# Warm-up matmuls in three groups of fixed size ahead of the first tiles of a fused attention and gated-FFN kernel

## The chip, the cores and the metric

One core of one Trainium2 chip. Kernels are compared only within the same rounds. The metric is the device time of one execution in microseconds (us). The profile's "span" of the same execution is about 1.7 us shorter than its time (562.7 and 564.47 us for the profiled execution of the kernel before), so the two are never mixed below.

## The reference

```python
xn = layernorm(x)                                   # x: 1 x 2048 x 576, bf16
s  = window_attention(xn, wqkv) @ wo                # 32 heads of 18, window 256
h  = sigmoid(xn @ w_gate) * (xn @ w_up)             # 576 -> 4608
g  = silu(h @ w_down)                               # 4608 -> 576
out = x + s * g
```

## The kernel before

The program is a list of operations with estimated durations; a greedy scheduler orders them for each engine, and the order is then emitted. The tokens come in four chunks of 512. In the first chunk, each block of 128 rows goes through this chain: DMA of x, statistics and normalisation (VectorE, with one power on GpSimd), PE transposes, a copy out of PSUM (ScalarE for the first three blocks, VectorE for the fourth). "F tiles" are the gate/up matmuls. The first two F tiles are cut into four parts of 128 columns, one for each block of rows, so that they can start before the whole chunk is there; all later F tiles have 512 columns.

While x and the first weights travel, PE runs filler matmuls on zeros, so that its clock is fast when real work comes. In the trace of before the filler pairs start 427 ns apart until 6.95 us, where the clock record goes to full speed, and 216 ns apart after it:

```python
NWARM = 36
FIRST_SLACK_NS = -900.0     # correction of the estimated landing of the first weights
TURN_NS = 215.0             # part of the estimate of each probability-value product
...
h = self.pool_f.hold()
w = None
for i in range(NWARM):
    def f_warm(eng):        # one "pair": two matmuls of 64 rows x 512 columns, started within 6 ns in the trace
        return pair(eng, self.halves(h, NT), lambda r, t: zero[r, :],
                    lambda r, t: zero[r, None, :].broadcast_to([SW, NT // P, P]), True, True)
    w = op("PE", 427 if i < 11 else 216, f_warm, f"warm:{i}", deps=[z], prio=4, acq=None if i else h, odeps=[w])
    w.filler = h
    h.release(w)
```

```python
# build_ln, first chunk: the transposes of one block of rows and the copy out of PSUM
tr = op("PE", KB * 29.5, f_tr, f"tr:{st}", deps=[ap, dup, self.op_ident, war], prio=0, acq=h)
...
xe = op(eng, ..., f_xe, f"xe:{st}", deps=[tr], prio=0)

# build_ffn, first chunk: two F tiles in four parts each
for ft, h in enumerate(hs):
    u = None
    for part in range(len(PARTS[ft])):
        lo = gate_up(ft, h, 0, None if part else h, part, [u])
        u = gate_up(ft, h, 1, None, part, [lo])

# schedule(): fillers that are left when the first F part is placed are dropped
if o.name.startswith("f1"):
    for d in [d for d in ops if d.filler is not None and d.idx < 0]:
        ...
```

So the number of fillers that are really emitted is a result of the scheduler's estimates: wherever it believes that PE would be idle, it puts one in. It came out as 13 pairs, then 8, then 2.

The softmax here doesn't subtract the row's maximum and nothing guards it: scores larger than these inputs give would overflow.

## Time and profile before

| | |
|---|---|
| time, 3 executions | 562.57, 562.66, 563.74 us |
| time of the profiled execution | 564.47 us (span 562.7 us) |
| PE busy | 556.2 us |

The profile's page of the kernel before: the span, PE's busy time and instruction count, the instruction queue of the DMA, and the chain of waits by engine.

```profile
span 562.7 us, 19207 instructions
...
PE 556.2 (99%) x8314; PEld 337.2 (60%) x8314; DVE 334.7 (59%) x793; ACT 271.5 (48%) x379; POOL 210.9 (37%) x358
...
q8 instruction: 65, 1.06, 0.8%
...
PE 98%; DVE 1%; issue 0%; DVEq 0%
```

PE is the bound. Fillers count as busy, though, so the page alone cannot show what they cost. For that one reads the order of events at the start. The timeline of PE in the kernel before; the columns are start, duration of the run of like instructions, operation, output and inputs, shape, count, and idle time before it with its releaser:

```profile
1.05 5.73 PE L109 MATMUL ps<-hT 64*128 64x512 bf16 x26 [1.05 <-DVE small L434]
6.57 0.48 PE L545 MATMUL ps<-ident,xnr 64*128 64x64 bf16 x10
6.86 1.93 PE L109 MATMUL ps<-hT 64*128 64x512 bf16 x16
8.62 0.31 PE L545 MATMUL ps<-ident,xnr 64*128 64x64 bf16 x10
8.77 0.59 PE L109 MATMUL ps<-hT 64*128 64x512 bf16 x4
9.20 0.22 PE L109 MATMUL ps<-xnT,wgr 64*128 64x128 bf16 x2
...
10.22 0.31 PE L545 MATMUL ps<-ident,xnr 64*128 64x64 bf16 x10
...
13.22 0.22 PE L109 MATMUL ps<-xnT,wgr 64*128 64x128 bf16 x2
13.28 0.56 PE L109 MATMUL ps<-xnT,wgs 64*128 64x128 bf16 x14
15.08 0.46 PE L109 MATMUL ps<-xnT,wgs 64*128 64x128 bf16 x10 [1.25 <-issue]
15.36 0.40 PE L109 MATMUL ps<-xnT,wgr 64*128 64x512 bf16 x2
```

`ps<-hT` are the fillers (26, 16 and 4 matmuls: 13, 8 and 2 pairs), `ps<-ident,xnr` the transposes, `ps<-xnT,...` the F tiles. The normalised rows of the first block were ready at 5.68 us and transposed at 6.57; the second at 7.29 and 8.62. The first F tile's weights had landed at 7.77 and it started at 9.20. And a wait of 1.25 us, put down to "issue", stands in the middle of a run of F matmuls. The waits of PE in the same trace (total, times, longest):

```profile
PE ps L109 <- issue: 1.2, 1, 1.2
PE ps L109 <- DVE small L434: 1.1, 1, 1.1
```

### The profile page before, as it was taken

How to read it: one execution, taken by the hardware profiler on the slowest of the kernel's cores; microseconds unless marked ns; L12 is line 12 of the kernel's file. 1: busy time of each engine (PE TensorE's matmuls, PEld its weight loads, DVE VectorE, ACT ScalarE, POOL GpSimd, SP SyncE). 2: the span in 40 equal slices, each digit the busy share in tenths (PEclk: the TensorE clock that was granted, in tenths of full speed). 3: DMA queues.
4: the chain of work that ended last, by engine and by line, in shares of the span. 5: the costliest groups of instructions: out<-in, count | busy, mean ns of one | idle time of the engine just before them, and what ended most of it. 6: DMA issues, size and time to landing. Idle time of an engine off the chain costs nothing.

```text
span 562.7 us, 19207 instructions
## 1 busy us (share of the span) xinstructions
PE 556.2 (99%) x8314; PEld 337.2 (60%) x8314; DVE 334.7 (59%) x793; ACT 271.5 (48%) x379; POOL 210.9 (37%) x358
## 2 busy tenths in 40 slices
PE   8999999999999999999999999999999999999997
PEld 5454454677775454565877566555477754444786
DVE  5467778778576876735785773586656133333133
ACT  2235565554556556556555645765754133223011
POOL 4565357664356635404675540366330100000000
PEclk9999999999999999999999999999999999999999
DMA  8976999631215455326411233444521026552010
GB/s 234 286 205 145 275 207 282 175 87 43 76 34 148 133 148 142 109 84 123 102 55 35 81 111 104 117 143 142 168 62 37 22 75 179 166 151 67 1 44 23
DMA packets 113323, 67.81 MB, mean 121 GB/s; under 512 B 18476, under 2 KB 111372, under 8 KB 113240
## 3 DMA queue, kind: packets, MB, share of 16 engines
q1 hardware_dynamic: 105816, 60.68, 39.4%
q0 software_dynamic: 7424, 5.92, 4.0%
q8 instruction: 65, 1.06, 0.8%
q14 instruction: 18, 0.15, 0.1%
HBM read 55.15 MB, written 2.36 MB: 102 GB/s over the span
## 4 chain that ended last, share of the span: by engine, by line
PE 98%; DVE 1%; issue 0%; DVEq 0%
PE ps L109 94%; PE ps L746 3%; DVE o2T L772 0%; DVE ot L764 0%; DVE s_attn L997 0%; DVE o L768 0%; DVE thf L1002 0%; DVE v_aug L644 0%; PE ps L545 0%; DVE xf L1007 0%; DVE ot L767 0%; DVE xnT L533 0%; DVE hT L433 0%; DVEq L1159 0%; DVE small L434 0%
## 5 line engine op out<-in xcount | busy, mean ns | idle before, releaser
L109 PE MATMUL ps<-xnT,wgs 64*128 64x512 bf16 (+1 forms) x2400 | 285.6, 368 | 1.3 <-issue 1.2
L696 ACT ACTIVATE expr<-ps 128x1024 bf16<-128x1024 f32 (+2 forms) x160 | 156.8, 980 | 86.7 <-PE ps L109 86.1
L109 PEld LDWEIGHTS ps<-xnT,wgs 64*128 64x128 bf16 x2400 | 113.8, 94 | 118.2 <-issue 1.4
L109 PE MATMUL ps<-wd_sb,hT 64*128 64x288 bf16 (+2 forms) x2448 | 154.3, 276 | 0.0
L892 DVE SCALAR_TENSOR_TENSOR hT<-tring,ps 128x512 bf16<-128x512 bf16 x144 | 98.2, 684 | 90.4 <-ACT tring L889 87.8
L889 ACT ACTIVATE tring<-ps 128x512 bf16<-128x512 f32 x144 | 85.8, 597 | 115.9 <-PE ps L109 114.2
L109 PEld LDWEIGHTS ps<-wd_sb,hT 64*128 64x128 bf16 x2448 | 113.1, 94 | 27.7
L265 POOL DMA_DIRECT2D qk<-qd x160 | 82.6, 523 | 109.0 <-PE ps L109 99.8
L709 DVE TENSOR_TENSOR expr<-expr,mask 128x256 bf16<-128x256 bf16 (+2 forms) x232 | 62.9, 302 | 53.6 <-ACT expr L696 53.0
L661 POOL TENSOR_SCALAR kx<-kprev,small 128x256 bf16<-128x256 bf16 x64 | 61.8, 974 | 32.1 <-PE ps L109 31.3
L265 POOL DMA_DIRECT2D oT<-o2T x72 | 37.0, 521 | 61.6 <-DVE o2T L772 52.3
L109 PE MATMUL ps<-qk,kx 64*128 64x320 bf16 (+4 forms) x736 | 59.8, 251 | 0.0
L109 PE MATMUL ps<-xnT,wgr 64*128 64x512 bf16 (+1 forms) x300 | 55.9, 368 | 0.3
L109 PEld LDWEIGHTS ps<-qk,kx 64*128 64x128 bf16 x736 | 32.1, 94 | 25.6 <-DVE hT L892 1.4
L109 PE MATMUL ps<-xnT,wqk 64*128 64x512 bf16 x256 | 32.7, 377 | 0.0
L764 DVE STREAM_TRANSPOSE ot<-ps 128x512 f32<-128x512 f32 x32 | 22.5, 702 | 13.3 <-PE ps L746 13.3
L987 ACT ACTIVATE thf<-ps 128x576 bf16<-128x576 f32 (+3 forms) x22 | 11.4, 520 | 35.5 <-PE ps L109 35.0
L583 DVE CAST qd<-ps 128x1024 bf16<-128x1024 f32 (+1 forms) x20 | 22.2, 1114 | 6.5 <-PE ps L109 6.3
L661 DVE TENSOR_SCALAR kx<-qk,small 128x512 bf16<-128x512 bf16 x64 | 22.5, 378 | 3.4 <-PE ps L109 3.1
L772 DVE STREAM_TRANSPOSE o2T<-o 128x512 bf16<-128x512 bf16 x32 | 22.8, 712 | 1.1
L817 ACT ACTIVATE s_attn<-ps 128x576 bf16<-128x576 f32 x16 | 9.9, 649 | 27.9 <-PE ps L109 27.9
L109 PEld LDWEIGHTS ps<-xnT,wgr 64*128 64x128 bf16 x300 | 15.0, 94 | 13.4 <-issue 1.1
(64 smaller groups left out, 305.3 us busy)
## 6 DMA issues: line engine op xcount, KB each, us to landing
wgs<-in_B_w_gate_dram SPq DMA_DIRECT2D x72, 256.0 KB, 3.3
wgs<-in_B_w_up_dram SPq DMA_DIRECT2D x72, 256.0 KB, 3.9
wd_sb<-in_B_w_down_dram SPq DMA_DIRECT2D x9, 576.0 KB, 6.0
qk<-qd POOLq DMA_DIRECT2D x100, 36.0 KB, 2.2
wgr<-in_B_w_gate_dram SPq DMA_DIRECT2D x36, 64.0 KB, 2.2
wgr<-in_B_w_up_dram SPq DMA_DIRECT2D x36, 64.0 KB, 2.3
xf<-in_A_x_dram SPq DMA_DIRECT2D x16, 144.0 KB, 2.3
out_dram<-xf SPq DMA_DIRECT2D x16, 144.0 KB, 1.8
```

Of the source, the lines that this page charges most:

```text
L109: res = eng.matmul(outs[i], lhs(ROWS[t], i), rhs(ROWS[t], i), start=start, stop=stop, tile_position=(64 * t, 0))
L265: o = self.op(eng, DMA_ISSUE_NS[eng], lambda e: e.dma_start(dst, src), name, deps, prio, nbytes=nbytes)
L583: return eng.tensor_copy(dst, self.both(h, n))
L661: return e.tensor_scalar(self.kx[:, sx, pos:pos + n_ // SW, t, :], src.rearrange("p (s k) -> p s k", k=SW), self.half[:, t:t + 1], None, A ...
L696: return eng.activation(self.expr[:, se, :, lo * SW:NT], self.both(h, NT)[:, :, lo * SW:NT], ACTF.Exp, scale=SM_SCALE)
L709: return eng.tensor_tensor(e_, e_, m_, ALU.mult)
L746: res = eng.matmul(outs[i][p0:p0 + VH, cols], self.v_aug[ROWS[i], o:o + VH], self.expr[ROWS[i], se, t, cols], start=n == 0, stop=n == len( ...
L764: return e.transpose(self.ot1[:, p1, :], self.halves(hp, NT)[i])
L772: t2 = op("DVE", dve_ns(NT), lambda e, p2=p2, p3=p3: e.transpose(self.o2T[:, p3, :], self.o2[:, p2, :]), f"ot2:{c}:{pr}:{i}", deps=[on, d3 ...
L889: th = op("ACT", act_ns(NT), lambda e: e.activation(self.tring[:, st, :], bank(h, 0), ACTF.Tanh, scale=0.5), f"th:{c}:{ft}", deps=[pg, dt_ ...
L892: mu = op("DVE", dve_ns(NT), lambda e: e.scalar_tensor_tensor(self.hT[:, ft, :], self.tring[:, st, :], 1.0, bank(h, 1), ALU.add, ALU.mult) ...
L987: return e.activation(v2(t)[:, a:b, :], y2()[:, a:b, :], ACTF.Tanh, scale=0.25)
```

## The change

The intent is to stop the scheduler from piling fillers up in front of work that is ready. There are now three groups of fixed size: 11 pairs ahead of the first transposes, 4 tied behind the first transposes, 1 behind the second. Three constants of the scheduler are set anew.

```diff
-TURN_NS = 215.0
+TURN_NS = 290.0
-NWARM = 36
+NWARM = (11, 4, 1)
-FIRST_SLACK_NS = -900.0
+FIRST_SLACK_NS = -970.0
@@ build_consts
-        z = op("DVE", 400, lambda e: e.memset(zero, 0.0), "init:zero", prio=0)
+        z = op("DVE", 920, lambda e: e.memset(zero, 0.0), "init:zero", prio=0)
-        h = self.pool_f.hold()
-        w = None
-        for i in range(NWARM):
-            ... (the loop shown above)
+        self.warm_h = self.pool_f.hold()
+        self.warm_src = zero
+        self.warm(NWARM[0], z, None, 427)
+    def warm(self, n, dep, before, est):
+        h, zero = self.warm_h, self.warm_src
+        def f_warm(eng): ... (as before)
+        for i in range(n):
+            w = self.op("PE", est, f_warm, f"warm:{i}", deps=[dep], prio=4, acq=None if before else h, odeps=[before])
+            w.filler = h
+            h.release(w)
+            before = w
@@ build_ln, behind each transpose of the first chunk
+            if i < 2:
+                self.warm(NWARM[1 + i], None, tr, 216)
```

## The prediction

> **What bounds the kernel.** TensorE: 556.2 of 562.7 us busy on the page; the chain of waits is 98% PE and from 16.7 to 557.4 us one unbroken run of matmuls, with 3 us of VectorE at the end. Time can be won where PE does filler, waits or runs slow: nearly all in the first 17 us, including waits of 1.25 us at 13.8 and 0.3 us at 12.6.

> **The start, from the timeline.** There are 23 warm-up pairs (46 records), spaced 427 ns until about 7.0 us and 216 ns after: thirteen ahead of the first transposes, eight before the second, two before the first F tile. The first rows are ready at 5.68 us, but PE, full of fillers, starts their transposes at 6.57. The second rows are ready at 7.29; transposed at 8.62. The first F tile's weights land by 7.77 and its activations (ScalarE's copy) at 7.79, yet its first matmul starts at 9.20. So 1.1 to 1.3 us of filler stands in front of ready work.

> **The change** fixes the fillers at 11, 4 and 1: 7 pairs fewer. Eleven slow pairs from 1.05 end near 5.75, as the first rows are ready. Transposes take 0.3 us of issue (still slow); four fillers, slow until about 7.0, end near 7.4; second transposes about 7.45, one filler to 7.8, first F matmul about 8.0, limited by weights at 7.77. The DMA order should stay.

> The 128-column parts take about 1 us per block of rows. Later blocks are then limited by VectorE (rows at 8.91 and 10.52): the fourth should start near 11.5 (12.93 before), and the parts finish near 12.5 (13.9 before, without the stall).

> **The 1.25 us wait** is put down to "issue": it falls inside an accumulation group where no semaphore is waited for, and a 16 KB packet on the instruction queue starts at 12.42 and takes 1.2 us while DMA is saturated. I read it as an instruction-fetch stall. With 28 fewer instructions before it, it moves to about the first 512-column tile, where instructions last longer. I expect 0.8 to 1.3 us. Later weights have slack (wqk lands at 19.55, used at 25.3), so the gain is kept.

> **The constants.** The estimate of the probability-value product grows by 75 ns (215 to 290), which only reorders the schedule. Its turnarounds lose about 280 ns each by matmul spacing (16 of them), so the estimate becomes truer; all other lost spacing after 50 us is about 1.5 us. I give this 0 plus or minus 0.5 us.

> **Clock.** [...] This trace turns fast 6.0 us after the first matmul. With fixed groups the start should depend less on this phase; the spread of before (562.57 to 563.74) may shrink.

> **Sum.** First F tile 1.2 us earlier, up to 1.5 us kept after the stall: 562.66 to **561.2 us**, range 560.4 to 562.3. Faster by over 2%: 0.005; within 2%: 0.99; slower: 0.005.

> **Signs.** First transposes near 5.75 us, second near 7.45, first F matmul near 8.0; first 512-column matmul before 14.3 (15.36 before); 16 warm-up pairs; one issue wait of about 1 us; PE after that as before.

> **What would make it wrong.** A longer fetch stall that eats the gain; a PE wait for weights or for the fourth rows; the clock turning fast later because fewer fillers keep PE busy; a reordered schedule with new waits in the attention.

## The result, and the profile after

| | kernel before | kernel after |
|---|---|---|
| median of 4 executions, us | 562.62 | 562.16 |
| range, us | 562.33 to 563.74 | 561.84 to 562.43 |
| ratio of the fast runs | | 0.9988 (95%: 0.9971 to 1.0005) |

A ratio is the mean time of one kernel's fast runs over that of the other's in the same rounds, so it is not quite the ratio of the medians quoted. The gain is 0.46 us by the medians and 0.7 us by the ratio. The predicted gain was 1.5 us. The interval contains 1: by these runs alone the gain is not certain.

The page of the kernel after, the same lines:

```profile
span 560.1 us, 19180 instructions
...
PE 553.5 (99%) x8300; PEld 335.7 (60%) x8300; DVE 335.7 (60%) x793; ACT 271.4 (48%) x379; POOL 210.8 (38%) x358
...
PE 97%; DVE 2%; DMA 0%; issue 0%; DVEq 0%
```

By these two traces the change looks like 2.6 us (562.7 to 560.1), four to six times what the times show. That gap was the first thing to explain. PE's timeline after, at the same places:

```profile
1.05 3.90 PE L109 MATMUL ps<-hT 64*128 64x512 bf16 x22 [1.05 <-DVE small L434]
5.72 0.32 PE L553 MATMUL ps<-ident,xnr 64*128 64x64 bf16 x10 [0.76 <-DVE xnr L518]
5.87 1.03 PE L109 MATMUL ps<-hT 64*128 64x512 bf16 x8
7.33 0.32 PE L553 MATMUL ps<-ident,xnr 64*128 64x64 bf16 x10 [0.43 <-DVE xnr L518]
7.49 0.38 PE L109 MATMUL ps<-hT 64*128 64x512 bf16 x2
7.87 0.23 PE L109 MATMUL ps<-xnT,wgr 64*128 64x128 bf16 x2
...
9.26 0.33 PE L553 MATMUL ps<-ident,xnr 64*128 64x64 bf16 x10
...
10.95 0.31 PE L553 MATMUL ps<-ident,xnr 64*128 64x64 bf16 x10
...
11.85 0.23 PE L109 MATMUL ps<-xnT,wgr 64*128 64x128 bf16 x2
...
12.88 0.38 PE L109 MATMUL ps<-xnT,wgr 64*128 64x512 bf16 x2
```

The start is as predicted: 22, 8 and 2 matmuls of filler, transposes at 5.72 and 7.33, first F matmul at 7.87, against 9.20. The waits of PE after:

```profile
PE ps L553 <- DVE xnr L518: 1.2, 2, 0.8
PE ps L109 <- DVE small L434: 1.0, 1, 1.0
```

The issue wait is gone, and PE now waits 1.2 us for VectorE's rows. These waits replace fillers and cost nothing by themselves: the first F matmul starts 0.14 us after the last of the first weights has landed (7.74 us). Everything after the first 512-column F matmul is practically unchanged: from there to the last matmul it takes 543.34 us before (15.36 to 558.69) and 543.18 us after (12.88 to 556.07). Beside the fillers, the traces show three differences in PE's order: the transposes of the third block stand one F part later (in after behind 46 F matmuls, at 9.26 us; in before behind 36, at 10.22 us), and two groups of eight matmuls with `wd_sb` have moved, near 295 and 443 us. The first of these comes back below.

### The profile page after: what moved, and what is told of

Read it like the earlier page. It is cut to its first block, busy times and chain, and to the rows that moved or that the text cites. A ratio compares the mean times of both kernels' runs of the same rounds, so it can differ in the third digit from the quotient of the medians.

```text
span 560.1 us, 19180 instructions
## 1 busy us (share of the span) xinstructions
PE 553.5 (99%) x8300; PEld 335.7 (60%) x8300; DVE 335.7 (60%) x793; ACT 271.4 (48%) x379; POOL 210.8 (38%) x358
## 3 DMA queue, kind: packets, MB, share of 16 engines
q0 software_dynamic: 7424, 5.92, 3.9%
## 4 chain that ended last, share of the span: by engine, by line
PE 97%; DVE 2%; DMA 0%; issue 0%; DVEq 0%
PE ps L109 93%; PE ps L754 3%; DMA x<-in_A_x_dram 0%; DVE o2T L780 0%; DVE ot L772 0%; DVE small L503 0%; DVE s_attn L1005 0%; DVE small L505 0%; DVE o L776 0%; DVE thf L1010 0%; DVE v_aug L652 0%; DVE xnr L515 0%; PE ps L553 0%; DVE xf L1015 0%; DVE ot L775 0%
## 5 line engine op out<-in xcount | busy, mean ns | idle before, releaser
L109 PEld LDWEIGHTS ps<-xnT,wgr 64*128 64x128 bf16 x300 | 15.0, 94 | 13.8 <-issue 1.3
```

What stands on the lines that cost most here:

```text
L109: res = eng.matmul(outs[i], lhs(ROWS[t], i), rhs(ROWS[t], i), start=start, stop=stop, tile_position=(64 * t, 0))
```

## The experiments

"Clock fast at" is where the trace's clock record goes to full speed. Theory A says that the first trace of before was an unlucky execution (clock fast late, and a wait for instructions), so the change's real worth is smaller than the traces say. Rival B says that the fillers always cost 1.2 us and something else gives it back later. Rival C says that the new constants, not the fillers, make the gain.

### 1. The two kernels again

**before_again**: no edit. Expected:

> The unchanged kernel before, for a second trace and more times. Theory A (an unlucky trace): the first trace of before (span 562.7) had the clock turn fast late (7.0 us) and a fetch stall of 1.25 us; its usual execution has a span near 561.0 (timed median 562.6 less the 1.7 us between time and span). So times again 562.3 to 563.8, ratio 1.000. If this trace has the clock fast by about 4.5 us, the first F matmul is near 8.2 us, not 9.2, and the fourth row block starts near 11.9; whether the stall is there decides the first 512-column matmul: 13.0 without, 14 or later with. Theory B (the fillers always cost 1.2 us): the first F matmul is at 9 us or later again.

Measured: 562.69 us median (562.51 to 563.09), span of the trace 561.0. The clock was fast at 6.04 us, not 6.95, there was no issue wait, and the start was:

```profile
6.31 0.31 PE L545 MATMUL ps<-ident,xnr 64*128 64x64 bf16 x10
...
8.18 0.31 PE L545 MATMUL ps<-ident,xnr 64*128 64x64 bf16 x10
...
8.76 0.22 PE L109 MATMUL ps<-xnT,wgr 64*128 64x128 bf16 x2
...
13.59 0.40 PE L109 MATMUL ps<-xnT,wgr 64*128 64x512 bf16 x2
```

The same kernel reaches its first 512-column tile 1.77 us sooner than in its first trace (13.59 against 15.36). So 1.77 of the 2.48 us between the first two traces at this point (15.36 to 12.88) was the execution, not the change. Rival B's "at 9 us or later" is missed.

**after_again**: no edit. Expected:

> The unchanged kernel after. Both theories: ratio 0.998 to 1.000 to before. Theory A: the first F matmul at 7.8 to 8.3 us whatever the clock's phase, the fourth row block near 11.85 (set by VectorE's rows), spread of times half of before's. If the fetch stall is a matter of luck and not of the change, it can show here too, as an issue wait of up to 1 us near 13 us.

Measured: 562.28 us median (562.09 to 562.77), ratio 0.9992 (0.9980 to 1.0004). First F matmul at 7.72, with the clock fast at 5.47 us, 1.64 us later than in the first trace of after (3.83): the start no longer depends on it. The kernel before, on the same chip in the same rounds, spread over 562.12 to 563.74 in 11 runs; but the five of before_again, the same kernel in the same rounds, spread over 0.58 us, less than the 0.68 us of the five here. Taking together the two sessions that ran after unchanged, their 20 fast times of before (before_again's among them) and 9 of after differ by 0.56 us in the mean, with a 95% interval of 0.26 to 0.86: the gain is small, but clear of zero. The issue wait appears here too, so the change does not remove it:

```profile
PE ps L109 <- DVE small L434: 1.0, 1, 1.0
PE ps L109 <- issue: 0.4, 1, 0.4
PE ps L553 <- DVE xnr L518: 0.4, 1, 0.4
```

### 2. Fillers or constants

**emit_13_8_2**: after's schedule, with the old numbers of pairs emitted.

```diff
+EXTRA = {11: 2, 4: 4, 1: 1}
+        def f_last(eng):
+            for _ in range(EXTRA[n]):
+                f_warm(eng)
+            return f_warm(eng)
         for i in range(n):
-            w = self.op("PE", est, f_warm, ...)
+            w = self.op("PE", est, f_last if i == n - 1 else f_warm, ...)
```

> The schedule and constants of after, but 13, 8 and 2 pairs emitted in the three groups, as in before; everything else in the same order. Theory A: as slow as before (ratio 0.999 to 1.001), because only the fillers and the instruction count matter; fetch stall back at 13 to 14 us where an early clock makes instructions run out earlier. Rival theory C (the gain comes from the constants and the reordered schedule): ratio as after, 0.998 to 0.999.

Measured: 563.85 us median, 562.13 to 567.72, ratio 1.0038 (1.0007 to 1.0069). Two of the six times were over 567 us at a mean clock of 0.997. The trace (clock fast at 5.48 us) has its first F matmul at 8.48 us.

**emit_again**: the same kernel.

> The run with 13, 8 and 2 pairs in after's order again, because two of its six times (567.4, 567.7, clock 0.997) were unlike all others. If those were chance, the times are now 562.1 to 564 and the ratio 0.999 to 1.0005, as before's; first F matmul between 8.2 and 9.3 by the clock's turn.

Measured: 563.57 us median (562.04 to 565.57), ratio 1.0003 (0.9980 to 1.0026). As slow as before, with after's constants and order; but the interval of the ratio also contains after's 0.9992, so the times alone do not exclude rival C. The traces do, as far as the start is concerned: with after's constants and the old numbers of fillers the first F matmul is at 8.48 and 8.98, not near 7.8. Here the clock was fast at 6.47 us. No time was over 565.6 us, so I count the two at 567 as disturbed executions; what disturbed them is open. The kernel before had one such time in these rounds (566.00 us at a clock of 0.997). The trace also has the longest issue wait of all, at the same kind of place:

```profile
13.29 0.56 PE L110 MATMUL ps<-xnT,wgs 64*128 64x128 bf16 x14
15.51 0.46 PE L110 MATMUL ps<-xnT,wgs 64*128 64x128 bf16 x10 [1.66 <-issue]
```

**old_constants**: after's fillers, the three constants of before.

```diff
-TURN_NS = 290.0
+TURN_NS = 215.0
-FIRST_SLACK_NS = -970.0
+FIRST_SLACK_NS = -900.0
-        z = op("DVE", 920, ...)
+        z = op("DVE", 400, ...)
```

> After with the three constants of before (215, -900, 400), fillers 11, 4, 1. Theory A: ratio as after (0.998 to 0.9995), the part after the first 512-column matmul within 0.3 us of after's 543.2 us to the last matmul. Theory C: ratio 1.000.

Measured: 563.33 us median (562.34 to 563.74), ratio 1.0004 (0.9992 to 1.0016). Theory A expected after's ratio; it missed, and rival C's number (1.000) is what came. The start is as after's (first F matmul 7.84, first 512-column matmul 12.64), but from there to the last matmul it takes 544.26 us, of which the issue wait takes about 0.3; the remaining 544.0 is 0.8 us more than after's 543.2. The scheduler is greedy, so the new start with the old constants gives another order for the rest, and in this trace that order costs what the start won. So rival C is wrong about the start, but right that the gain is not kept with every order of the rest.

**turn215**: after with only the product's estimate at the old 215 ns.

```diff
-TURN_NS = 290.0
+TURN_NS = 215.0
```

> After with only the product's estimate back at 215 ns. The PE order then differs from after's in 180 lines, while the order of before and of after differ in the fillers alone. Theory: the new estimate is needed only to get the old order back with the new start, so this kernel loses what the run with all three old constants lost: first 512-column matmul near 12.7 to 12.9 us, but 543.7 to 544.3 us from there to the last matmul (after: 543.2), ratio 1.000 to 1.001. Rival (the estimate does nothing): ratio 0.999 as after.

Measured: 562.70 us median (561.61 to 563.17), ratio 0.9994 (0.9981 to 1.0008). From the first 512-column matmul to the last it takes 542.86 us, 0.3 less than after. My theory that the larger estimate is needed fell. The loss of old_constants must come from the other two constants, or from all three together; this was not divided further. (The recorded text says that the orders of before and after differ in the fillers alone; the three moves named above are left out there.) What the traces show is that the order of the rest moves the time by some tenths of a microsecond either way, not that 290 is a better number than 215. By the times alone none of these runs stands apart from before, except emit_13_8_2 with its two odd times; the reading rests on the traces.

### 3. The issue wait

**split_fillers**: each filler pair as two pairs of 256 columns, 64 more PE instructions at the same filler time.

```diff
-            return pair(eng, self.halves(h, NT), ...broadcast_to([SW, NT // P, P]), True, True)
+            for half in range(2):
+                o = pair(eng, [b[:, 256 * half:256 * half + 256] for b in self.halves(h, NT)], lambda r, t: zero[r, :],
+                         lambda r, t: zero[r, None, :].broadcast_to([SW, 2, P]), True, True)
+            return o
```

> After with each filler pair split into two pairs of 256 columns: same filler time, same order, 64 more PE instructions ahead of the first F tile. Fetch theory: the dry point moves forward to about 12.1 us (record 448 falls where record 384 was), inside the 128-column parts; the packet is asked for earlier as well, so the wait is 0 to 1 us, but it sits 64 instructions earlier in the program than in the other traces of after. If the wait is not fetch: it stays at the same matmul (the first full F tile) or is absent.

Measured: 562.67 us median (562.51 to 563.20), ratio 1.0000 (0.9986 to 1.0015). There was no issue wait in the trace, which both theories allow, so for the fetch question it is inconclusive. It showed something else: the first weights landed at 8.42 us instead of about 7.75, and with the fillers gone PE waited for them:

```profile
PE ps L109 <- DVE small L434: 1.1, 1, 1.1
PE ps L109 <- DMA wgr<-in_B_w_up_dram: 0.8, 1, 0.8
```

First F matmul 8.56. In before_again the same weights landed at 8.40, and nobody noticed, because the fillers ran until 8.76.

**single_fillers**: each pair as one matmul of 128 rows, 32 fewer PE instructions at the same filler time.

```diff
-            return pair(eng, self.halves(h, NT), ...)
+            return eng.matmul(self.halves(h, NT)[0], zero, zero[:, None, :].broadcast_to([P, NT // P, P]), start=True, stop=True)
```

> After with each filler pair (two matmuls of 64 rows at once) made one matmul of 128 rows: same filler time, same order, 32 fewer PE instructions ahead of the first F tile. Fetch theory (PE runs dry after a fixed number of instructions, about record 448 of the trace, and waits for a 16 KB instruction packet): the dry point moves into the 512-column tiles, near 14.6 to 15 us, and the packet is usable 2.3 to 2.8 us after its start near 11.2 us, so the issue wait of up to 0.8 us goes in nearly all runs: ratio 0.998 to 0.999, fewer times above 562.4, no wait in the trace. If the wait is not fetch: as after, a wait in about half the traces.

Measured: 562.36 us median (561.81 to 563.32), ratio 0.9993 (0.9980 to 1.0006). No issue wait near 14 us, as expected, but the times did not come down, and the trace has one at 366 us:

```profile
365.52 1.03 PE L109 MATMUL ps<-xnT,wgs 64*128 64x512 bf16 x7
366.98 0.37 PE L109 MATMUL ps<-xnT,wgs 64*128 64x512 bf16 x1 [0.44 <-issue]
```

Its place tells what the wait is likely to be. Counting the records of PE in each trace (matmuls, weight loads, semaphore waits) up to the last one ahead of the wait:

| trace | fillers | wait at, us | gap between records, us | records ahead of it |
|---|---|---|---|---|
| before | 13, 8, 2 | 13.6 | 1.46 | 449 |
| emit_again | 13, 8, 2 | 13.6 | 1.87 | 449 |
| after_again | 11, 4, 1 | 12.95 | 0.81 | 449 |
| old_constants | 11, 4, 1 | 12.9 | 0.49 | 449 |
| single_fillers | 11, 4, 1 single | 366.2 | 0.81 | 11,201 = 449 + 42 x 256 |

### 4. What the four and the one are for

**thin_between**: the second and third group cut from 512 to 16 columns.

```diff
+            if est < 300:
+                return pair(eng, self.halves(h, 16), lambda r, t: zero[r, :], lambda r, t: zero[r, 0:16], True, True)
```

> After with the four and the one filler pair cut from 512 to 16 columns, so that PE is nearly idle between the first transposes and the first F tile. If these fillers only keep the clock: where the clock has turned fast before about 5.8 us, nothing changes (first F matmul about 7.75 to 7.9, by its weights); where it has not, it turns later and the first blocks of F run at half speed, up to 2 us longer. Over runs a wider spread upwards, median ratio 0.999 to 1.002. If they do nothing: as after in all runs.

Measured: 563.20 us median (562.73 to 563.56), ratio 0.9991 (0.9970 to 1.0013) in rounds where before itself was noisy (562.59 to 566.00). Four of its five times have a mean clock of 0.996 or 0.997. Stretches of its trace (busy time and count of PE, PEld, DVE, ACT, POOL, then granted clock, DMA share, GB/s), and then the same stretches of after:

```profile
6.00:8.00 2.00, 0.51 (x26) 0.35 (x20) 1.93 (x8) 0.99 (x2) 0.88 (x2) 0.96 0.91 252
8.00:10.00 2.00, 2.00 (x40) 2.00 (x42) 1.27 (x6) 0.41 (x1) 0.77 (x2) 0.50 0.94 276
10.00:12.00 2.00, 2.00 (x57) 1.92 (x54) 0.75 (x10) 0.70 (x1) 1.37 (x2) 0.69 1.13 296
```

```profile
6.00:8.00 2.00, 1.57 (x30) 0.58 (x23) 1.93 (x8) 1.01 (x2) 0.90 (x2) 1.00 0.80 231
8.00:10.00 2.00, 2.00 (x78) 1.91 (x75) 1.27 (x6) 0.77 (x2) 0.75 (x2) 1.00 0.99 284
10.00:12.00 2.00, 1.80 (x64) 1.45 (x62) 1.22 (x11) 0.33 (x1) 1.39 (x2) 1.00 0.98 276
```

The clock was fast at 4.43 us, PE was then busy for a quarter of the stretch from 6 to 8 us, and the clock record shows half speed for 3,413 ns, from 7.85 to 11.26 us. (The fast stretches in the records of before and after are 163 times as long, 556,372 ns each.) PE ran 40 matmuls from 8 to 10 us instead of 78. The first 512-column matmul came at 14.27 us instead of 12.88. My expectation ("nothing changes where the clock has turned before 5.8") was wrong: the clock had turned, and was lost again. So by this trace, and by the lower clock in four of the five times, the four and the one pay for themselves; the ratio cannot tell this run from after. The longest single gap ahead of the loss was 1.21 us, against 0.76 us in after, where the clock stayed. Over the 3,413 ns from the clock's turn to its loss (4.43 to 7.85 us) PE was busy for 46%; in after, over the same length from its turn (3.83 to 7.25 us), for 68%. Over the 3,413 ns ahead of the turn in after (0.42 to 3.83 us) PE was busy for 82%; from 0.12 to 3.53 us in before it was busy for 73%, and the clock turned only one such stretch later, at 6.95. That the busy share over such a stretch decides, and not the one gap, is my estimate from these four shares; with one trace of thin_between it is not shown.

### 5. Where the remaining waits come from, and a better version

In after's order PE stands still twice more, 0.23 us ahead of the third block and 0.32 us ahead of the fourth (by the waits of its weight loads; the fourth block's rows are there at 10.49, and its transposes start at 10.95):

```profile
10.31 0.18 DVE L518 COPY xnr<-xnr 128x64 bf16<-128x64 bf16 x1
10.38 0.10 PEld L109 LDWEIGHTS ps<-xnT,wgr 64*128 64x128 bf16 x2 [0.23 <-ACT xnT L541]
...
11.85 0.10 PEld L109 LDWEIGHTS ps<-xnT,wgr 64*128 64x128 bf16 x2 [0.32 <-DVE xnT L541]
```

In four traces of it (after, after_again, single_fillers, split_fillers) the first 512-column tile starts 5.01 us after the first F matmul, against 4.83 in before_again. The order makes this difference, not the number of fillers: emit_13_8_2, with the old fillers in after's order, takes 5.00 us.

**tr_moves**: the transposes of the third and the fourth block one F part earlier in PE's order, after scheduling. For the third block this is the place that they have in before.

```diff
+    def reseat(self):
+        pe = self.prog["PE"]
+        for name, k in (("tr:2", 4), ("tr:3", 9)):
+            parts = [o for o in pe if o.name in ("f10:0:0", "f11:0:0", "f10:0:1", "f11:0:1")]
+            t = pe.pop(next(i for i, o in enumerate(pe) if o.name == name))
+            pe.insert(pe.index(parts[k]), t)
```

> After with only two transposes moved in the PE order: the third one F part earlier (ahead of the second block's first part), the fourth one part earlier. In every trace of after's order the time from the first F matmul to the fourth block is 3.98 us, with waits of 0.22 and 0.31 us, while the fourth rows have been ready since 10.44. Placement theory (the waits come from transposes standing too close ahead of the block that uses them): both waits go or nearly so, first F to fourth block 3.5 to 3.7 us, first 512-column matmul about 0.4 us earlier for the same landing of the first weights, ratio 0.998. My earlier theory (VectorE's rows set the fourth block): about 3.95 us again, ratio as after (0.999).

Measured: the five fast runs took 561.69 to 563.37 us, ratio 0.9975 (0.9955 to 0.9996). The profiled execution was slow (2,594 us; after the first, a filler pair every 1.28 us or more), so there is no usable trace, and whether exactly the two waits went is not shown for this kernel.

**reseat_single**, and the same again as **reseat_again**: single fillers, the transposes of the third block two F parts earlier than in after and those of the fourth one part earlier (the recorded text says two for both), and the small column copies of the first chunk on ScalarE.

```diff
+            def f_dup(e, sn=sn):
+                if e is self.nc.scalar:
+                    return e.activation(self.xnr[:, sn, 0:RD], self.xnr[:, sn, RD:2 * RD], ACTF.Copy)
+                return e.tensor_copy(self.xnr[:, sn, 0:RD], self.xnr[:, sn, RD:2 * RD])
+    def reseat(self):                      # after scheduling
+        for i in range(4):
+            ...                            # ln:dup:i from VectorE's order to ScalarE's, ahead of the copy that follows
+        for name, k in (("tr:2", 3), ("tr:3", 9)):
+            ...                            # as in tr_moves
```

> A candidate better than both: single fillers; the four small copies that duplicate 64 columns of the rows move from VectorE to ScalarE; the third and fourth transposes move two F parts earlier in the PE order; the rest keeps after's order. Theory (VectorE's rows set the fourth block in after): rows ready about 0.4 us sooner for the third and 0.6 for the fourth block, first F matmul still near 7.8 (weights), fourth block near 11.1 to 11.3 (after 11.85), first 512-column matmul near 12.1 to 12.3 (after 12.8), kept to the end: ratio 0.9975 to 0.9985. Rival (something else sets the fourth block): first 512-column matmul 12.7 or later, ratio as after.

Measured: four fast runs, 561.39 to 561.82 us, ratio 0.9978 (0.9964 to 0.9993). The profiled execution was slow (724 us at a granted clock of 0.75) and is left out.

> The candidate again (single fillers, copies on ScalarE, both transposes earlier), because its trace fell in a slow execution (724 us, clock 0.75). Expected: ratio 0.9975 to 0.9985 again; first F matmul 7.7 to 7.9, fourth block about 3.6 us later, no issue wait before the second 512-column tile. If tr_moves gains as much, the copies and single fillers add nothing that shows.

Measured: 561.55 us median (561.43 to 561.71), ratio 0.9963 (0.9944 to 0.9982); before in those rounds was at 563.33, above its usual 562.6, so the first run's 0.9978 is the safer number. Its timeline:

```profile
7.92 0.23 PE L109 MATMUL ps<-xnT,wgr 64*128 64x128 bf16 x2
...
8.70 0.33 PE L555 MATMUL ps<-ident,xnr 64*128 64x64 bf16 x10
...
10.46 0.32 PE L555 MATMUL ps<-ident,xnr 64*128 64x64 bf16 x10
...
12.48 0.38 PE L109 MATMUL ps<-xnT,wgr 64*128 64x512 bf16 x2
```

From the first F matmul to the first 512-column one it takes 4.56 us instead of 5.01, with no wait between them. All nine fast executions of this version lie within 561.39 and 561.82 us: it is faster than before by about 0.2%, and below all nine fast times of after (561.84 to 562.77), by about 0.1%; the latter is indirect, as no round ran both. Which of its three edits does how much was not divided, except that tr_moves alone gave 561.69 to 563.37, so the moves are probably most of the mean and do not explain the narrow spread.

## Why the prediction was right or wrong

The time fell into the predicted range and the mechanism at the start held; the gain was 0.5 to 0.7 us and not 1.5. The range was met only just, and partly by luck: 562.16 against an upper end of 562.3, in reach of the unchanged kernel as well (562.12 in one of its 11 later times). Going through the sum:

**"First F tile 1.2 us earlier."** Right for the trace it was read from (9.20 to 7.87), too large as a typical value. This is the term that was mis-sized. With 13, 8 and 2 fillers the first F matmul depends on when the clock turns fast:

| trace with 13, 8, 2 | clock fast at, us | first F matmul, us |
|---|---|---|
| emit_13_8_2 | 5.48 | 8.48 |
| before_again | 6.04 | 8.76 |
| emit_again | 6.47 | 8.98 |
| before (the first trace) | 6.95 | 9.20 |

Each microsecond of lateness costs 0.49 us, since fillers take 427 ns on the slow clock and 216 ns on the fast one. With 11, 4 and 1 pairs of the same kind (after, after_again, old_constants, turn215) the clock turned at 3.83, 5.47, 5.92 and 6.86 us and the first F matmul came at 7.87, 7.72, 7.84 and 7.98. Twelve fast traces turned at 5.8 us on average (3.83 to 6.95, all with the first matmul at 1.05 us), which by the first table means a first F matmul near 8.6. The usual gain at this point is therefore about 0.8 us. That is still a little high: in all eight traces with the new groups the first F matmul comes 0.13 to 0.14 us after the last of the first weights has landed, and in two of the twelve traces these landed late (8.40 and 8.42 us). With the mean landing of all twelve, 7.86 us, my estimate is 8.0 for the first F matmul and a gain of about 0.6 us. The first trace of before had the latest clock of all twelve.

**"Four fillers, slow until about 7.0, end near 7.4."** That carried the phase of one trace over to another kernel's execution. The turn was at 3.83 us in the trace of after. It made no difference, because rows and weights set the start.

**"The fourth block should start near 11.5", limited by VectorE.** It started at 11.85. Rows were ready at 10.49, as the prediction had it, but their transposes came at 10.95: the limit is the place of the transposes in PE's order. The loss is 0.18 us in the time to the first 512-column tile, counted against before_again; it came in with the new schedule, which put the transposes of the third block one F part later. So VectorE's rows were the wrong limit for this step, in the prediction and in my first theory.

**"The 1.25 us wait ... I read it as an instruction-fetch stall."** Supported by the 449 and the 42 x 256 records; what makes the packet late is open. But the prediction counted on improving it by up to 0.3 us, as if it happened in every execution. It happens in some executions of either kind: in two of the four traces with 13, 8 and 2 pairs (1.25 and 1.66 us of idle time) and in two of the four with 11, 4 and 1 (after, after_again, old_constants, turn215; at most 0.44 us). Those are too few to call a difference.

**"The constants: 0 plus or minus 0.5."** Held. After's order is the same as before's but for the fillers and three moves, and it keeps the rest at 543.2 us; one other set of constants lost 0.8 us in its trace, and another gained 0.3.

**"The gain is kept."** Right: no wait for later weights appeared.

**"The spread of before may shrink."** Not shown. In the same rounds it was 562.12 to 563.74 us before (11 runs) against 562.09 to 562.77 after (5 runs), but the five of before_again lie within 562.51 to 563.09, closer together than after's five. What the traces above do show is that the start itself depends less on the clock.

Added up from typical values: about 0.6 to 0.8 us at the first F matmul, less 0.18 at the transposes, gives about 0.45 to 0.6 us, against a measured 0.46 by the medians, 0.7 and 0.45 us by the two ratios, and 0.56 us over all times. No hidden give-back is needed. The warning was there beforehand: the profiled execution took 564.47 us and the median was 562.66, so 1.8 us of that trace were not typical, and a late clock plus a 1.25 us stall was where to look.

Still open: what the narrow spread of the last version comes from, which of the constants makes old_constants slower, why an instruction packet starts late in some executions, and what the odd executions at 567, 724 and 2,594 us were.

## What to carry to other kernels

Before costing a step from one trace, compare the time of the profiled execution with the median; if it lies outside the spread, part of what the trace shows is that execution alone. Put no more filler ahead of ready work than the gap needs, but keep some in every gap: here too much filler on a slow clock put the first F matmul anywhere from 8.48 to 9.20 us, and too little lost the clock for 3.4 us. When filler goes, the next limits come up in turn, here the landing of the first weights, the place of the transposes in the order, and the instruction stream itself.
